# The out projection of a gated layer in seven half-depth products, with stationary weights and moving h

## The chip, the cores and the metric

One core of a Trainium2 chip runs the whole program. The metric is device time in microseconds, lower is better. Times are given as the median of the runs; the profile is of one more execution.

## The reference

Performer attention over 8 batches, 8 heads, 576 positions and head size 64 is followed by a gated feed-forward layer over all 4608 tokens, all in float32:

```python
q_p, k_p = phi(q_s), phi(k_s)              # random features, 128 of them
kv = einsum('bhsm,bhsd->bhmd', k_p, v)
num = einsum('bhsm,bhmd->bhsd', q_p, kv); den = ...
x = num / den                              # laid out as (4608, 512)
xn = x / sqrt(mean(x * x) + 1e-06) * rms_g
g = xn @ w_gate                            # (4608, 512) @ (512, 1536)
val = xn @ w_val
out = (g * sigmoid(g) * val) @ w_out       # (4608, 1536) @ (1536, 512)
```

The weights come as float64-like raw words of 8 bytes and are turned into float32 on the chip. Each float32 operand of a matmul is split into a high part (rounded to the matmul's float32r type) and a low part (the rest), and each product takes three matmuls: high x high, high x low, low x high (`three_pass`).

## The kernel before, in words

Tokens are cut into 12 blocks of 384 (`NBLK`, `TB`), DFF = 1536 into 12 rows of 128 (`NF`), DM = 512 into 4. There are three stages.

Stage A does the attention, normalises x, transposes it (`xT`, and a copy in HBM, `xn_scratch`) and computes the first six rows f of the gated layer (`gated`, `FA` = 6) in ordinary products: weights stationary, 384 tokens moving. Each h row goes to HBM, `h_scratch`. In the same stage `weights(n)` loads all 36 weight tiles of 128 x 512, turns them into float32 on ScalarE and VectorE, and keeps the first 12 split in SBUF. The next 12 pass through `sums`: four sums and differences of their halves are made on VectorE (`sr`), and the seven left-hand factors go to HBM, `lw_scratch`. The last 12, the rows of w_out, are stored as they are to `wo_scratch`.

Stage B computes the other six rows of gate and value (`right`, `left`, `unit`) by the Strassen-Winograd scheme: blocks are taken in pairs (`bp`, six of them), and a 2 x 2 arrangement (two row halves of the product, two halves of the contraction, two blocks) is made with seven products of half the depth in place of eight. `ORDER` lists which left factor meets which right factor. `right` loads four quarters of xn, makes the differences t1 to t4 on VectorE and splits the seven right factors with `halve`: a high part cast by ScalarE, a low part subtracted by VectorE. The results are the R tiles, one pair (high, low) for each of the seven names. `unit` runs the seven products of 6 matmuls each, into three PSUM banks a, b, c; ScalarE copies partial results m1, m5, u2 out of PSUM, VectorE adds them to later ones (`total`). Silu and the product of gate and value follow, and h goes to `h_scratch`.

Stage C is the out projection in ordinary products. `out_weights(f)` loads row f of w_out from HBM and splits it: row 0 into the pool wo0, the others into wo. `out_tile(blk, f)` loads h of one block and row (128 x 384), splits it, and makes 9 matmuls: for each of three groups of 128 tokens, h is stationary and 512 columns of w_out move, three passes, into a PSUM bank that is summed over f. After f = 11 the three banks are copied out (VectorE, ScalarE) and stored as rows of the output.

SBUF is laid out in groups of pools (`GROUPS`). Groups named in `RIGHT` are laid from the top end downwards, the others from the bottom upwards. The very first on the right is "edge", a tile of 8 floats that nobody uses. `change` frees groups and enters new ones in the same place when the items it lists are done: `to_b` and `in_b` lead to stage B. For stage C `to_c` replaces "sources" (xn quarters, raw left factors) by "first" once the last right factors are made, and `in_c` replaces "products" (with the left factors lw of units 1 to 5) by "last" once everything of stage B is done, its last store included. Left factors of unit 0 lie on the right, in lw0, inside the group "operands", as do the R tiles.

The order of all engines' work is made by `Plan` when the program is built: every item has an engine, an assumed duration, items it comes after, a key (smaller first) and buffers that it takes and gives back; a list simulation emits the instructions in the order in which they would begin. Each engine then runs its own instructions strictly in that order, and all loads and stores are issued by SP.

Of the kernel before, what the change touches and what calls it, by code (L numbers as in the profile page):

```python
# [9 lines left out]
F32 = mybir.dt.float32  # L10
F32R = mybir.dt.float32r
AF = mybir.ActivationFunctionType
ALU = mybir.AluOpType
# [16 lines left out]
FA = 6  # L30
# [54 lines left out]
LAND = 2.2  # L85
# [3 lines left out]
class Plan:  # L89
# [95 lines left out]
def performer_glu_kernel(  # L185
# [11 lines left out]
    xn_d: bass.AP,  # L197
    h_d: bass.AP,
    lw_d: bass.AP,
    wo_d: bass.AP,  # L200
):
    nc = tc.nc
    ve = nc.vector
# [53 lines left out]
    def tile_(pool, shape, name, dtype=F32, tag=None):  # L257
        return pools[pool].tile(shape, dtype, tag=tag or pool, name=name)
# [7 lines left out]
    def weights(n, key):  # L266


        if n < 2 * NF:
            src = wgv[n // 2, n % 2]  # L270
        else:
            src = wout[n - 2 * NF]
        t = {}

        def load():
# [56 lines left out]
        if n >= 2 * FA:  # L332

            st["wt", n] = t
            if n >= 2 * NF:

                def store():
                    nc.sync.dma_start(wo_d[n - 2 * NF], t["w"])

                i = st["wo", n - 2 * NF] = add("SP", 0.26 / RATE, store, [i], key, land=LAND)  # L340
                add("NONE", 0, lambda: None, [i], give=[("w", n)])
            else:
                st["w", n] = i
                if n % 4 > 1:
                    sums(n, key)
            return
        f, j = n // 2, n % 2

# [15 lines left out]
    def sums(n, key):  # L364

        un = (n - 2 * FA) // 4 * 2 + n % 2
        t = {}

        def add_up(i):
            def go():  # L370
                if i == 0:
                    t["s"] = tile_("sr", [P, 4, 2 * P], f"sr{un}")
                a, b, s = st["wt", n - 2]["w"], st["wt", n]["w"], t["s"]
                half = slice(0, 2 * P), slice(2 * P, DM)
                x, y, op = (
                    (b[:, half[0]], b[:, half[1]], ALU.add),
                    (s[:, 0], a[:, half[0]], ALU.subtract),
                    (a[:, half[0]], b[:, half[0]], ALU.subtract),
                    (a[:, half[1]], s[:, 1], ALU.subtract),
                )[i]  # L380
                ve.tensor_tensor(out=s[:, i], in0=x, in1=y, op=op)

            return go

        def store(i):
            def go():
                if i == 0:
                    a = st["wt", n - 2]["w"]
                    nc.sync.dma_start(lw_d[un, :, 0:2], a.rearrange("p (i k) -> p i k", i=2))
                elif i == 1:  # L390
                    nc.sync.dma_start(lw_d[un, :, 2], st["wt", n]["w"][:, 2 * P : DM])
                else:
                    nc.sync.dma_start(lw_d[un, :, 3:7], t["s"])

            return go

        after = [st["w", n - 2], st["w", n]]
        ends = [add("SP", size / RATE, store(i), after[i : i + 1], key, land=LAND) for i, size in ((0, 0.26), (1, 0.13))]
        for i in range(4):
            after = [add("DVE", 0.42, add_up(i), after, key, [] if i else [("sr", un)])]  # L400
        ends.append(add("SP", 0.52 / RATE, store(2), after, key, land=LAND))
        st["lw", un] = ends
        add("NONE", 0, lambda: None, ends, give=[("w", n - 2), ("w", n), ("sr", un)])

    def features(tag, c, key):

# [476 lines left out]
    def unit(bp, fp, j, key):  # L883
# [63 lines left out]
        p4 = mm(5, "c", [p3], True)  # L947
        c11 = total("c11", "c", "m1", [p4, m1], [("psB", at, "c"), ("m1", at)])
        p6 = mm(6, "a", [p4, c22], False)
        st["t", bp, un] = t  # L950
        for nm, done in (("c12", c12), ("c22", c22), ("c11", c11), ("c21", p6)):
            src = "a" if nm == "c21" else nm
# [41 lines left out]
    for bp in range(NBLK // 2):  # L994
        for un in range(NU):
            unit(bp, un // 2, un % 2, base + NU * bp + un)

    to_c = change(users("sources"), ["sources"], ["first"])
    in_c = change(list(range(to_c)), ["products"], ["last"])

    def out_weights(f, key):
        t = {}

        def load():
            t["raw"] = tile_("wst", [P, DM], f"oraw{f}")
            nc.sync.dma_start(t["raw"], wo_d[f])

        def hi(part="h"):
            if (f, part) not in lw:
                pool = pools["wo" if f else "wo0"]  # L1010
                lw[f, part] = pool.tile([P, DM], F32R, name=f"o{part}{f}")
            return lw[f, part]

        ready = [in_c if f else to_c]
        i = add("SP", 0.26 / RATE, load, [st["wo", f], to_c], key, [("wst", f)], land=LAND)
        raw = lambda: t["raw"]
        st["o", f] = halve("DVE", hi, lambda: hi("l"), raw, key, [i] + ready, DM, give=[("wst", f)])

    def out_tile(blk, f, key):
        t = {}  # L1020
        at = (blk, f)

        def load():
            t["raw"] = tile_("hin", [P, TB], f"hC{blk}_{f}")
            nc.sync.dma_start(t["raw"], h_d[blk, :, f])

        def hi():
            if "h" not in t:
                t["h"] = tile_("hs", [P, TB], f"hh{blk}_{f}", F32R)
                t["l"] = tile_("hs", [P, TB], f"hl{blk}_{f}", F32R)  # L1030
            return t["h"]

        def product():
            if f == 0:
                st["po"] = [tile_("psB", [P, DM], f"po{blk}_{c}") for c in range(NC)]
            for c in range(NC):
                cs = slice(c * P, (c + 1) * P)
                three_pass(
                    nc,
                    st["po"][c],  # L1040
                    [(t["h"][:, cs], t["l"][:, cs], lw[f, "h"], lw[f, "l"])],
                    start=(f == 0),
                    stop=(f == NF - 1),
                )
            st["po", blk] = st["po"]

        def leave_psum(c):
            def go():
                t["o"] = tile_("o", [P, DM], f"o{blk}_{c}")
                if c % 2 == 0:  # L1050
                    ve.tensor_copy(t["o"], st["po", blk][c])
                else:
                    nc.scalar.copy(t["o"], st["po", blk][c])
                t["o", c] = t["o"]

            return go

        def store(c):
            r0 = blk * TB + c * P
            return lambda: nc.sync.dma_start(out[r0 : r0 + P, :], t["o", c])  # L1060

        i = add("SP", 0.2 / RATE, load, [st["hs", at], to_c], key, [("hin", at)], land=LAND)
        i = halve("DVE", hi, lambda: t["l"], lambda: t["raw"], key, [i], TB, [("hs", at)], [("hin", at)])
        take = [("psB", blk, c) for c in range(NC)] if f == 0 else []
        before = [st["made"]] if "made" in st else []
        i = add("PE", 2.06, product, before + [i, st["o", f]] + ([in_c] if f else []), key, take, [("hs", at)])
        st["made"] = i
        if f == NF - 1:
            for c in range(NC):
                eng, dur = ("ACT", 0.6) if c % 2 else ("DVE", 0.7)  # L1070
                ps, o = ("psB", blk, c), ("o", blk, c)
                n = add(eng, dur, leave_psum(c), [i], key - 1000, [o], [ps])
                add("SP", 0.26 / RATE, store(c), [n], key - 1000, give=[o], land=LAND)

    base = 12000
    for f in range(NF):
        out_weights(f, base + f)
    for blk in range(NBLK):
        for f in range(NF):
            out_tile(blk, f, base + blk * NF + f + 0.5)  # L1080
# [69 lines left out]
```

## Time and profile before

| | us |
|---|---|
| median of 3 runs | 1181.23 (1179.86 to 1181.67) |
| the profiled execution | 1181.44 |
| its span, first to last instruction | 1177.9 |
| busy: TensorE / VectorE / ScalarE / GpSimd | 1161.9 / 674.7 / 580.2 / 131.8 |
| mean granted TensorE clock | 0.998 |
| stage A, to the first product of stage B | 0 to 600.3 |
| stage B, to the first product of stage C | 600.3 to 869.3 |
| stage C, to the end of the span | 869.3 to 1177.9 |

How to read it: the execution's own time is 3.5 us longer than the span of its instructions. A matmul's busy time is its latency, and matmuls overlap, so the pace of TensorE is read from the starts of neighbouring matmuls and not from their durations. A line of the profile can be that of a helper (`three_pass` has L179 to L181, `halve` L789 and L794), and the tile's name tells the use: po is the out projection, pa, pb, pc are the products of stage B, ff those of stage A.

### The profile page before, as it was taken

The page shows a single profiled execution, that of the slowest core. Times are in us where ns is not written, and L with a number is a line of the kernel's source. Part 1 is how long each engine was busy: PE and PEld are TensorE (multiplying, and loading weights), DVE is VectorE, ACT ScalarE, POOL GpSimd, SP SyncE. Part 2 cuts the span into 40 slices and gives each one's busy share as a digit, 9 for nine tenths or more (in the row PEclk, how much of TensorE's full clock was granted, in tenths as well). Part 3 has the DMA queues.
Part 4 walks back from the last instruction along what each step waited for, and adds up shares of the span by engine and source line. Part 5 has one row for each costly group of instructions (what it writes and reads, how often), then busy time and mean ns, then how long its engine had stood idle before and what let it go on. Part 6 is the DMA issues. An engine that isn't in the chain of part 4 may idle for free.

```text
span 1177.9 us, 19998 instructions
## 1 busy us (share of the span) xinstructions
PE 1161.9 (99%) x7433; PEld 1067.4 (91%) x7433; DVE 674.7 (57%) x1390; ACT 580.2 (49%) x1418; POOL 131.8 (11%) x170
## 2 busy tenths in 40 slices
PE   9999999999999999999989999999999999999998
PEld 6898999999999999999989999999988888888886
DVE  4889887998787755547324664664553333333332
ACT  5777777766755655545145454454442222222221
POOL 0133111020201111224144000000000000000000
PEclk9999999999999999999999999999999999999999
DMA  8665585686565633316223331331444444444442
GB/s 285 222 206 176 175 257 178 195 266 212 168 207 170 204 109 100 96 62 222 85 67 106 106 107 63 100 107 54 161 128 135 121 121 147 121 121 121 121 121 86
DMA packets 98032, 171.14 MB, mean 145 GB/s; under 512 B 9360, under 2 KB 65552, under 8 KB 97936
## 3 DMA queue, kind: packets, MB, share of 16 engines
q1 hardware_dynamic: 97712, 169.58, 45.2%
q8 instruction: 58, 0.95, 0.3%
q10 hardware_dynamic: 224, 0.30, 0.1%
q14 instruction: 38, 0.31, 0.1%
HBM read 114.00 MB, written 55.84 MB: 144 GB/s over the span
## 4 chain that ended last, share of the span: by engine, by line
PE 51%; DVE 2%; DMA 0%; issue 0%; ACT 0%; ACTq 0%; DVEq 0%
PE po L180 9%; PE po L179 8%; PE po L181 8%; PE pa L179 4%; PE pa L181 4%; PE pa L180 4%; PE pb L181 2%; PE pb L180 2%; PE pb L179 2%; PE ff L179 1%; PE ff L181 1%; PE ff L180 1%; PE pc L181 1%; PE pc L180 1%; PE pc L179 1%; DMA h_scratch<-h 0%
## 5 line engine op out<-in xcount | busy, mean ns | idle before, releaser
L179 PE MATMUL ff<-xhi,whi 128*128 128x384 f32 x576 | 200.5, 348 | 2.7 <-DVE u L720 2.7
L181 PE MATMUL ff<-xhi,wlo 128*128 128x384 f32 x576 | 193.1, 335 | 0.0
L180 PE MATMUL ff<-xlo,whi 128*128 128x384 f32 x576 | 192.8, 335 | 0.0
L794 DVE TENSOR_TENSOR hl<-hC,hh 128x384 fp32r<-128x384 f32 x144 | 80.2, 557 | 186.4 <-ACT hh L789 186.4
L179 PE MATMUL po<-oh,hh 128*128 128x512 f32 x432 | 170.3, 394 | 1.4 <-ACT oh L789 1.4
L789 ACT CAST hh<-hC 128x384 fp32r<-128x384 f32 x144 | 74.1, 515 | 196.8 <-PE po L180 195.3
L180 PE MATMUL po<-ol,hh 128*128 128x512 f32 x432 | 170.3, 394 | 0.2 <-DVE ol L794 0.2
L181 PE MATMUL po<-oh,hl 128*128 128x512 f32 x432 | 170.1, 394 | 0.0
L179 PEld LDWEIGHTS ff<-xhi,whi 128*128 128x128 f32 x576 | 108.2, 188 | 6.5 <-DVE u L720 3.7
L180 PEld LDWEIGHTS ff<-xlo,whi 128*128 128x128 f32 x576 | 108.4, 188 | 0.0
L181 PEld LDWEIGHTS ff<-xhi,wlo 128*128 128x128 f32 x576 | 108.1, 188 | 0.0
L179 PEld LDWEIGHTS po<-oh,hh 128*128 128x128 f32 x432 | 80.8, 187 | 21.6 <-ACT oh L789 1.8
L180 PEld LDWEIGHTS po<-ol,hh 128*128 128x128 f32 x432 | 80.8, 187 | 20.1 <-DVE ol L794 0.5
L181 PEld LDWEIGHTS po<-oh,hl 128*128 128x128 f32 x432 | 80.8, 187 | 19.8
L463 ACT ACTIVATE qp<-pjq,biq 128x128 f32<-128x128 f32 x288 | 80.7, 386 | 17.4 <-DVE biq L454 14.8
L463 ACT ACTIVATE kp<-pjk,bik 128x128 f32<-128x128 f32 x288 | 79.8, 388 | 18.5 <-DVE bik L454 14.0
L662 POOL TENSOR_TENSOR xlo<-xr,xhi 128x512 fp32r<-128x512 f32 x36 | 47.2, 1312 | 323.5 <-ACT xhi L659 323.5
L716 ACT ACTIVATE t<-ff 128x384 f32<-128x384 f32 x72 | 35.4, 491 | 90.1 <-PE ff L181 90.1
L924 DVE TENSOR_TENSOR c<-pb,u 128x384 f32<-128x384 f32 x36 | 20.0, 556 | 88.4 <-PE pb L181 82.9
L593 PE MATMUL nu<-kv,qpT 128*128 128x65 f32 (+1 forms) x640 | 68.8, 264 | 0.0
L593 PEld LDWEIGHTS nu<-kv,qpT 128*128 128x128 f32 (+1 forms) x640 | 66.2, 181 | 2.4 <-issue 0.6
L720 DVE SCALAR_TENSOR_TENSOR u<-t,ff 128x384 f32<-128x384 f32 x72 | 39.6, 550 | 48.4 <-ACT t L716 48.0
(145 smaller groups left out, 2254.5 us busy)
## 6 DMA issues: line engine op xcount, KB each, us to landing
hC<-h_scratch SPq DMA_DIRECT2D x144, 192.0 KB, 2.4
ink<-in_kx_dram SPq DMA_DIRECT2D x36, 512.0 KB, 4.3
inq<-in_qx_dram SPq DMA_DIRECT2D x36, 512.0 KB, 4.0
h_scratch<-h SPq DMA_DIRECT2D x72, 192.0 KB, 1.9
h_scratch<-c SPq DMA_DIRECT2D x72, 192.0 KB, 1.9
f<-in_wgv_dram SPq DMA_DIRECT2D x24, 512.0 KB, 3.9
xn_scratch<-xr SPq DMA_DIRECT2D x36, 256.0 KB, 2.8
Xb<-xn_scratch SPq DMA_DIRECT2D x24, 384.0 KB, 3.6
```

The source lines that it names most:

```text
L179: nc.tensor.matmul(out, lhsT=ah, rhs=bh, start=first, stop=False, skip_group_check=again)
L180: nc.tensor.matmul(out, lhsT=ah, rhs=bl, start=False, stop=False, skip_group_check=again)
L181: nc.tensor.matmul(out, lhsT=al, rhs=bh, start=False, stop=last, skip_group_check=again)
L463: nc.scalar.activation(st[tag + "p", c][:, h, :], t["pts"][h % 2][:, h // 2, :], AF.Exp, bias=t["bi"][:, h : h + 1], scale=SCALE,)
L593: nc.tensor.matmul(pt[lo:hi, i, :], lhsT=t["qpT"][:, h, lo:hi], rhs=st["kv", b][:, h, :], start=True, stop=True,)
L662: nc.gpsimd.tensor_tensor(out=st["xT", blk][1][:, :, cs], in0=t["xr"], in1=st["xT", blk][0][:, :, cs].bitcast(F32), op=ALU.subtract,)
L716: nc.scalar.activation(t["t"], t[0], AF.Tanh, scale=0.5)
L720: ve.scalar_tensor_tensor(out=t["u"], in0=t["t"], scalar=1.0, in1=t[0], op0=ALU.add, op1=ALU.mult)
L789: h = add("ACT", 0.1 + size / 970, lambda: nc.scalar.copy(hi(), raw()), after, key, take)
L794: e.tensor_tensor(out=lo(), in0=raw(), in1=hi().bitcast(F32), op=ALU.subtract)
L924: ve.tensor_tensor(out=t[name], in0=t[bank], in1=t[y], op=ALU.add)
```

## The change

Stage C is made by the scheme of stage B. The left-hand, stationary factors are combinations of quarters of w_out (rows f and f + 6 are the two halves of the contraction, columns 0 to 255 and 256 to 511 the two row halves of the result). They are made by `sums` in stage A, which now serves both sets of weights, stores three quarters as they are and the four sums together, and for w_out writes them to `wl_scratch`; rows f and f + 6 are loaded one after the other. The right-hand, moving factors are quarters of h of a pair of blocks, [128, 2 rows, 384] at a time (index g, three for each quarter), loaded by `out_right`, with differences t1 to t4 on VectorE, t1, t3 and t4 in place of their sources. Each is split with `halve` into one of the seven R tiles, which are taken in turn. `out_weights(n)` loads the factor of product n (all six f at once) and splits it: product 0 into the tiles of lw0, once unit 0 of the last pair is done, the others into "last". `out_pair` makes, for each product and each g, 6 matmuls of 384 columns for each of two column groups u; ScalarE copies k1, k5, k2 and the last result out of PSUM, VectorE adds the other three. The result is the output transposed, stored as 128 x 384 pieces; the host turns it back. The edge tile grows from 8 to 24 floats.

```diff
-    pools["edge"].tile([P, 8], F32, name="edge")
+    pools["edge"].tile([P, 24], F32, name="edge")
...
-    "first": {"hin": (6, 1), "hs": (3, 2), "wst": (4, 1), "wo0": (1, 1)},
-    "last": {"wo": (1, 1), "o": (3, 1)},
+    "first": {"hb11": (3, 1), "hb12": (3, 1), "hb22": (3, 1), "ht2": (3, 1), "wst": (2, 1)},
+    "last": {
+        "wo": (1, 1), "hb21": (3, 1), "k1": (2, 1), "k5": (2, 1), "k2": (2, 1), "o": (6, 1),
+    },
...
-            src = wout[n - 2 * NF]
+            src = wout[(n - 2 * NF) // 2 + NU * (n % 2)]
...
+            if n < 2 * NF and n % 4 > 1:
+                sums(n - 2, n, (n - 2 * FA) // 4 * 2 + n % 2, key)
+            elif n >= 2 * NF and n % 2:
+                sums(n - 1, n, (n - 2 * NF) // 2, key)
...
         def store(i):
             def go():
+                if i < 3:
+                    a11, a12, _, a22 = parts()
+                    to = wl_d[i, :, un] if out else lw_d[un, :, i]
+                    nc.sync.dma_start(to, (a11, a12, a22)[i])
+                elif out:
+                    nc.sync.dma_start(wl_d[3:7, :, un].rearrange("i p k -> p i k"), t["s"])
...
+    def out_weights(n, key):
+        i = ORDER[n][0]
+        size = 1 if n == 0 else 2
+        def load():
+            t["raw"] = tile_("wst", [P, NU, 2 * P], f"oraw{i}")
+            nc.sync.dma_start(t["raw"], wl_d[i])
...
+            deps = [ld, st["lw0"] if n == 0 else in_c]
+            e = halve("DVE", ..., deps, size * 2 * P)
...
+    def out_right(bp, key):
+        place = {"t1": "b11", "t3": "b12", "t4": "t2"}
...
+        def halves(n, g, after):
+            k = (NBLK // 2 * 7 + 21 * bp + 3 * n + g) % 7
+            slot = "R" + ORDER[k][1]
...
+        for g in gs:
+            halves(0, g, [ld["b11", g]])
+        for g in gs:
+            sub("t1", g, "b12", "b11", [ld["b12", g], e["b11", g]], 2.5)
+            halves(1, g, [d["t1", g]])
+        for g in gs:
+            sub("t2", g, "b22", "t1", [ld["b22", g], d["t1", g]], 4)
+            halves(2, g, [d["t2", g]])
...
+    def out_pair(bp, key):
+        def product(n, u, g, bank, first):
...
+                for k in range(2):
...
+                    pairs.append((wh, wl, r["h"][:, k], r["l"][:, k]))
+                three_pass(
+                    nc, t[bank, u], pairs, start=first, stop=(g == NU // 2 - 1), again=True
+                )
...
+        banks = "ababaca"
+        for n in range(7):
+            for g in range(NU // 2):
+                for u in range(2):
+                    deps = [st["RO", bp, n, g]]
+                    if bp == 0:
+                        deps += [st["o", n, 2 * g], st["o", n, 2 * g + 1]]
...
-    args.append(nc.dram_tensor("out_0_dram", (B * S, DM), F32, kind="ExternalOutput").ap())
+    args.append(nc.dram_tensor("out_0_dram", (DM, B * S), F32, kind="ExternalOutput").ap())
...
-    return r.results[0]["out_0_dram"]
+    return np.ascontiguousarray(r.results[0]["out_0_dram"].T)
```

More of the change, by code (lines that the diff above doesn't have):

```diff
@@ L395, in store @@
             return go
-        after = [st["w", n - 2], st["w", n]]
-        ends = [add("SP", size / RATE, store(i), after[i : i + 1], key, land=LAND) for i, size in ((0, 0.26), (1, 0.13))]
+        after = [st["w", m], st["w", n]]
+        ends = [add("SP", 0.4, store(i), after, key, land=LAND) for i in range(3)]
         for i in range(4):
[L400 to L403, printed above, removed]
+            after = [add("DVE", 0.42, add_up(i), after, key, [] if i else [("sr", m)])]
+        ends.append(add("SP", 0.52 / RATE, store(3), after, key, land=LAND))
+        st["wl" if out else "lw", un] = ends
+        add("NONE", 0, lambda: None, ends, give=[("w", m), ("w", n), ("sr", m)])
     def features(tag, c, key):
@@ L996, in performer_glu_kernel @@
             unit(bp, un // 2, un % 2, base + NU * bp + un)
+    st["lw0"] = st["lw0", NBLK // 2 - 1]
     to_c = change(users("sources"), ["sources"], ["first"])
     in_c = change(list(range(to_c)), ["products"], ["last"])
-    def out_weights(f, key):
+    lo_w = {}
+    def out_weights(n, key):
         t = {}
+        i = ORDER[n][0]
+        size = 1 if n == 0 else 2
         def load():
[L1005 to L1017, printed above, removed]
@@ new lines, in load, with piece @@
+            nc.sync.dma_start(t["raw"], wl_d[i])
+        after = [x for f in range(NU) for x in st["wl", f]] + [to_c]
+        ld = add("SP", 0.79 / RATE, load, after, key, [("wst", n)], land=LAND)
+        ends = []
+        for f0 in range(0, NU, size):
+            def piece(part, f0=f0):
+                if (n, f0, part) not in lo_w:
+                    if n == 0:
+                        w = pools["lw0"].tile(
+                            [P, 1, 2 * P], F32R, tag=f"lw0_{f0}{part}", name=f"o{part}{i}_{f0}"
+                        )
+                    else:
+                        w = pools["wo"].tile([P, 2, 2 * P], F32R, name=f"o{part}{i}_{f0}")
+                    lo_w[n, f0, part] = w
+                return lo_w[n, f0, part]
+            deps = [ld, st["lw0"] if n == 0 else in_c]
+            raw = lambda f0=f0: t["raw"][:, f0 : f0 + size]
+            e = halve(
+                "DVE", lambda p=piece: p("h"), lambda p=piece: p("l"), raw,
+                key + 0.01 * f0, deps, size * 2 * P,
+            )
+            for f in range(f0, f0 + size):
+                st["o", n, f] = e
+            ends.append(e)
@@ new lines, in out_pair, with go, copy @@
+    def out_pair(bp, key):
+        t = {}
+        def product(n, u, g, bank, first):
+            def go():
+                if first:
+                    t[bank, u] = tile_("psB", [P, DM], f"q{bank}_{bp}_{u}")[:, :TB]
+                r = st["ro", bp, n, g]
+                pairs = []
+                for k in range(2):
+                    f = 2 * g + k
+                    f0 = f if n == 0 else 2 * g
+                    wh, wl = (
+                        lo_w[n, f0, p][:, f - f0, u * P : (u + 1) * P] for p in "hl"
+                    )
+                    pairs.append((wh, wl, r["h"][:, k], r["l"][:, k]))
+                three_pass(
+                    nc, t[bank, u], pairs, start=first, stop=(g == NU // 2 - 1), again=True
+                )
+            return go
+        def copy(name, bank, u):
@@ L1063, in out_tile @@
[L1063 to L1073, printed above, removed]
@@ L1075, in performer_glu_kernel, with finish, go @@
-    base = 12000
[L1076 to L1080, printed above, removed]
+                t[name, u] = tile_(name, [P, TB], f"{name}_{bp}_{u}")
+                nc.scalar.copy(t[name, u], t[bank, u])
+            return go
+        def finish(nm, bank, y, u):
+            def go():
+                o = t[nm, u] = tile_("o", [P, TB], f"o{nm}_{bp}_{u}")
+                if y is None:
+                    nc.scalar.copy(o, t[bank, u])
+                else:
+                    ve.tensor_tensor(out=o, in0=t[bank, u], in1=t[y, u], op=ALU.add)
+            return go
```

185 lines of the change are left out of this document (129 added, 56 removed).

## The prediction

> **What bounds the kernel now.** I read the engine table first, then the chain of waits, then busy time by stretches cut where the stages change.
>
> ```profile
> span 1177.9 us, 19998 instructions
> PE 1161.9 (99%) x7433; PEld 1067.4 (91%) x7433; DVE 674.7 (57%) x1390; ACT 580.2 (49%) x1418; POOL 131.8 (11%) x170
> PE 51%; DVE 2%; DMA 0%; issue 0%; ACT 0%; ACTq 0%; DVEq 0%
> ...
> 300.00:420.00 120.00, 120.00 (x945) 116.71 (x945) 94.34 (x219) 71.45 (x186) 20.44 (x27) 1.00 0.57 183
> 600.30:650.00 49.70, 46.01 (x252) 45.26 (x253) 17.26 (x29) 30.27 (x72) 26.50 (x35) 0.97 0.31 104
> 650.00:869.32 219.32, 219.32 (x1261) 218.95 (x1261) 124.39 (x205) 96.98 (x183) 0.00 (x0) 1.00 0.29 96
> 869.32:896.66 27.34, 25.71 (x109) 20.23 (x109) 14.39 (x25) 12.18 (x24) 0.00 (x0) 1.00 0.54 161
> 896.66:1173.45 276.79, 276.79 (x1189) 222.04 (x1187) 85.90 (x152) 72.29 (x142) 0.00 (x0) 1.00 0.41 121
> ```
>
> The stretches list length, then busy time and count of PE, PEld, DVE, ACT, POOL, then clock and DMA. TensorE is never idle for long, the clock is full, and the chain names hardly anything but matmuls. So time is the number of matmuls times the spacing from start to start. The out projection runs from 869.32 to 1173.45: 27.34 + 276.79 = 304.1 us for 1296 matmuls of 512 columns. Stage B, already in seven half-depth products, has 1512 of 384 columns.
>
> ```profile
> 650.01 0.35 PE L179 MATMUL pb<-Rt1h,lw_3h 128*128 128x384 f32 x1
> 650.20 0.34 PE L180 MATMUL pb<-Rt1l,lw_3h 128*128 128x384 f32 x1
> 650.37 0.34 PE L181 MATMUL pb<-Rt1h,lw_3l 128*128 128x384 f32 x1
> 650.55 0.33 PE L179 MATMUL pb<-Rt1h,lw_3h 128*128 128x384 f32 x1
> 650.73 0.33 PE L180 MATMUL pb<-Rt1l,lw_3h 128*128 128x384 f32 x1
> ...
> 672.09 0.34 PE L179 MATMUL pa<-Rb11h,lw_0h 128*128 128x384 f32 x1
> 679.37 0.34 PE L179 MATMUL pa<-Rb11h,lw_0h 128*128 128x384 f32 x1
> ...
> 879.62 0.40 PE L181 MATMUL po<-oh,hl 128*128 128x512 f32 x1
> 896.42 0.40 PE L181 MATMUL po<-oh,hl 128*128 128x512 f32 x1
> ...
> 897.36 0.39 PE L179 MATMUL po<-oh,hh 128*128 128x512 f32 x1
> 898.72 0.39 PE L179 MATMUL po<-oh,hh 128*128 128x512 f32 x1
> ```
>
> These rows of the timeline carry the spacings. 672.09 and 679.37 are the first matmuls of two neighbouring units, 42 matmuls apart: 173.3 ns each. From 879.62 to 896.42 lie 72 steps of the out projection: 233.3 ns. From 897.36 to 898.72 lie six: 226.7 ns. So 128 more columns cost 53.3 ns, and 13.3 ns a matmul do not depend on its width; most out-projection matmuls pay 6.7 ns on top.
>
> Where do the 6.7 ns come from? The six fast steps are those of row f = 0, whose weights (wo0) lie in a right-hand pool; the others' lie in wo, left-hand. In the built kernel left-hand tiles of stages B and C start at multiples of 128 bytes, and right-hand ones 64 bytes off, since 32 bytes of "edge" lie above them. Write each pair as (moving, stationary), modulo 128: out projection f > 0 is (0, 64), f = 0 is (64, 64); stage B is (64, 0) for units 1 to 5 and (64, 64) for unit 0. Only (0, 64) costs the 6.7 ns. A change from (64, 0) to (64, 64) stretches four spacings: 650.01 to 650.73 is 0.72 us where four make 0.693, so 27 ns once.
>
> **The change part by part.** *Matmuls.* Seven products x 6 row tiles x 2 column halves x 3 passes = 252 per pair of blocks, six pairs: 1512, at N = 384. At 173.3 ns that is 262.1 us against 304.1, **-42.0 us**, if nothing waits. Fewer columns (580,608 against 663,552) would make 0.875 of the time; 262.1/304.1 is 0.862, because the 6.7 ns and 2.2 us of waits at the old start (next fence) go too, less the 13.3 ns on 216 more matmuls.
>
> *Alignment.* The edge grows from 32 to 96 bytes, every right-hand tile moves 64, and all pairs of stages B and C become (0, 0). The trace has no such pair. Bounds: the three good readings, and stage A whose two operands both stand 32 off, at 173.3 (rows below), say equal offsets are the cheap case; the one bad reading, +6.7 ns, also is the only one with a moving operand at 0. I take **173.3**, nearest to (64, 64) and (32, 32), and keep ±6.7 ns on 3024 matmuls, ±20.2 us, for the rivals. The 27 ns stretches go: some 20 of them, **-0.5**.
>
> ```profile
> 590.11 0.33 PE L179 MATMUL ff<-xhi,whi 128*128 128x384 f32 x1
> 599.30 0.34 PE L181 MATMUL ff<-xhi,wlo 128*128 128x384 f32 x1
> ...
> 872.96 0.50 PE L179 MATMUL po<-oh,hh 128*128 128x512 f32 x1 [1.40 <-ACT oh L789]
> 873.69 0.50 PE L180 MATMUL po<-ol,hh 128*128 128x512 f32 x1 [0.23 <-DVE ol L794]
> ...
> 870.21 1.91 DMA h_scratch<-c
> 872.29 0.63 ACT oh L789
> 872.94 0.70 DVE ol L794
> ```
>
> (53 steps between the first two: 173.4 ns.) The Trainium skill (TensorE: Matmul & The Clock Gate, Part 2) says the stationary and the moving operand come through two independent read ports, so that loading weights takes nothing from a running matmul; the 6.7 ns, which depend on the pair, do not fit that. The Trainium skill (same page, Back-to-back issue gap) gives N/2.4 + 2.5 ns, 162.5 ns at 384 columns, which no pair here reaches; were the aligned pair to reach it, the sum below would be lower by 10.8 ns x 3024 = 32.7 us, an estimate by that page.
>
> *The start of stage C.* The last rows are the chain there: the last store of stage B lands at 872.1, only then do the pools change, and wo's first tile is cast and split. TensorE lost 2.2 us. Now product 0 has its weights in lw0's tiles (free after unit 0 of the last pair, 869.3 - 5 x 7.28 = 832.9) and h in the R tiles, which come free product by product in the last unit, every 1.04 us from 862.0 + 1.04 = 863.1; its 36 matmuls are 6.2 us of cover, to 875.5. Product 1's first weights can be ready at 872.3 + 0.62 + 0.69 = 873.6. The cover holds; without it, the old 2.2 us.
>
> *Supply of h.* This is the new load.
>
> ```profile
> L849 DVE TENSOR_TENSOR Xt<-Xb,Xt 128x768 f32<-128x768 f32 x12 | 11.9, 989 | 0.2
> L794 DVE TENSOR_TENSOR Rb11l<-Xb,Rb11h 128x768 fp32r<-128x768 f32 x6 | 5.7, 958 | 14.1 <-ACT Rb11h L789 14.1
> L794 DVE TENSOR_TENSOR Rb21l<-Xb,Rb21h 128x768 fp32r<-128x768 f32 x6 | 6.4, 1064 | 0.0
> L789 ACT CAST Rt4h<-Xt 128x768 fp32r<-128x768 f32 x6 | 5.0, 840 | 1.7 <-PE pa L180 1.7
> L924 DVE TENSOR_TENSOR c<-pb,u 128x384 f32<-128x384 f32 x36 | 20.0, 556 | 88.4 <-PE pb L181 82.9 <-ACT lw_3h L789 4.7 <-DMA oraw<-wo_scratch 0.4
> L917 ACT COPY m<-pa 128x384 f32<-128x384 f32 x36 | 17.3, 480 | 52.3 <-PE pa L181 52.2
> L794 DVE TENSOR_TENSOR ol<-oraw,oh 128x512 fp32r<-128x512 f32 x12 | 8.1, 690 | 8.6 <-ACT oh L789 8.6
> L789 ACT CAST oh<-oraw 128x512 fp32r<-128x512 f32 x12 | 7.2, 618 | 10.0 <-DMA h_scratch<-c 6.4 <-DMA oraw<-wo_scratch 3.5
> ```
>
> Per pair VectorE has 21 low halves x 0.96 + 12 differences x 0.99 + 6 totals x 0.56 = 35.4 us; ScalarE 21 casts x 0.84 + 8 copies x 0.48 = 21.5; TensorE 252 x 0.1733 = 43.7. So VectorE fills 81% of each pair, and the seven R slots hold 14.6 us of matmuls ahead. In steady state TensorE sets the pace.
>
> Not in the first pair. Three-quarters of stage C's weights are split then too: 18 x 0.69 = 12.4 us on VectorE, which cannot start before 872. Count VectorE from 864.2 (first R tile free at 863.1, its cast 0.84, some 0.2 for the hand-overs): product 0's low halves 2.9 and stage B's last seven totals 3.9, done at 871.0; product 1, 3 x (0.69 + 0.99 + 0.96) = 7.9, at 878.9; product 2 at 886.8; product 3 (no difference) 4.95, at 891.8; product 4 at 899.7; a pair of totals 1.1; product 5 at 905.7; totals 1.1; product 6 at 914.7, or 915.8 if totals go first. TensorE wants the last third of product n at 869.3 + 6.24n + 4.16: 879.7, 886.0, 892.2, 898.4, 904.7, 910.9. It is late by 0.8 at product 2, 1.3 by product 4 and **4 us** by product 6. Lower end 0.5 (VectorE starts earlier), upper 8 (handshakes with ScalarE 10% longer). In the second pair VectorE's 8 us of slack pays it back.
>
> *PSUM.* Copies and totals of 0.48 and 0.56 have one whole product, 6.24 us, before their bank is written again: nothing.
>
> *Loads and stores.* Weights of one product are 768 KB into two buffers; half as much takes 3.6 us and 512 KB 4.5, so I estimate 6 to 7 us, with two products' time to come: nothing. Bytes per pair: 12 loads of 384 KB and 8 stores of 192 KB, 6.3 MB in 43.7 us, 144 GB/s where the first rows show 217 moved under full TensorE.
>
> ```profile
> wr<-lw_scratch SPq DMA_DIRECT2D x6, 512.0 KB, 4.5
> Xb<-xn_scratch SPq DMA_DIRECT2D x24, 384.0 KB, 3.6
> ...
> 0.00:300.00 300.00, 296.36 (x2461) 270.90 (x2461) 243.69 (x562) 218.21 (x623) 51.05 (x68) 1.00 0.67 217
> ...
> L338 SPq DMA_DIRECT2D wo_scratch<-w x12: 319/320/424, 339.9 to 416.4; - x12
> L838 SPq DMA_DIRECT2D Xb<-xn_scratch x24: 319/320/577, 535.8 to 787.7; - x24
> L381 DVE TENSOR_TENSOR sr<-w x6: 417/422/426, 196.5 to 334.5; 128x256 f32<-128x256 f32 x6
> ```
>
> *Sums of the out weights.* 24 adds x 0.42 = 10.1 us on VectorE; SP issues 24 stores in place of 12 and, for the gate and value weights, 24 in place of 18: 18 x 0.32 = 5.8 us more. All this lies near 340 to 480. From 300 to 420 VectorE has 94.3 of 120 us busy and TensorE all of it, and stage B's first loads, which wait until these tiles are given up, go out at 535.8. Hidden; without cover 10 us. I add **+0.5** for a reshuffled order, ends -1 and +5.
>
> *The end.* A ScalarE copy of 0.48 and 192 KB replace a VectorE copy of 0.69 (L1051, 128x512) and 256 KB: **-0.3**.
>
> Sum: 1181.4 (the profiled execution, 0.2 above the median 1181.23) - 42.0 - 0.5 + 4.0 + 0.5 - 0.3 = **1143 us**; with its ends 1137 to 1152.
>
> **The rivals.** (a) *Aligned pairs are cheaper than any seen*: if the step from (0, 64) to (64, 64) happens once more, 6.7 ns x 3024: 1123. For it: 13.3 ns remain unexplained in every spacing. Against: three different pairs share exactly this value, like a floor. By the Trainium skill's gap, cited above, it would be 1110, an estimate.
>
> (b) *The moving operand at 0 is what costs*: +6.7 ns x 3024, stage B slows too: 1163. For it: the only slow pair has it. Against: an effect of one operand would hardly let the weights' offset leave its mark in the 27 ns stretches.
>
> (c) *VectorE becomes the bound in every pair.* It needs 8.3 us more than 35.4; with all low halves at 1.06, as Rb21l's mean, it is 37.5, still short. At 48 us per pair: 1143 + 6 x 4.3 = 1169.
>
> (d) *Slower than before: each low half waits out its cast.* If VectorE cannot start a half until its own cast is done and the cast does not run ahead, a pair takes 21 x (0.84 + 0.96) + 11.9 + 3.3 = 53.0 us: 318 against 304.1, with weights split in series (24 pieces, near 28 us) in the first pair 1195 to 1223. It decides from 304.1/6 = 50.7 us a pair. Against: before Rb21l VectorE stood idle 0.0 us, so casts run ahead; with seven slots they can again.
>
> **How the numbers follow.** Forecast 67%, (a) 14%, (b) 8%, (c) 7%, (d) 4%. The range 1119 to 1158 holds the forecast, most of (a) and the mild end of (c); (b), (d) and the far ends of (a) and (c) stay out, some 20%. The forecast's own range is 1137 to 1152. A measurement here tells 0.2%, 2.4 us; all but (d) are faster: 0.96, 0.01, 0.03.
>
> **What would show it.** Right: 1512 matmuls of 384 columns in stage C spaced 173.3 ns; stage B as before without stretched spacings; idle time before matmuls only in the first pair of C, released by VectorE's low halves or weights, about 4 us; no wait for a copy or total; stage B starting near 600. Wrong: a spacing of 166.7 or 180.0 in B and C alike (a, b); idle time before matmuls in every pair (c, d); stage B starting several us later.

## The result, and the profile after

| | before | after |
|---|---|---|
| median of 4 runs each, us | 1180.74 (1179.86 to 1181.67) | 1144.08 (1143.85 to 1145.20) |
| ratio | | 0.9691, interval 0.9675 to 0.9708 |
| profiled execution, us | 1181.44 | 1143.85 |
| its span, us | 1177.92 | 1142.07 |

The forecast was 1143.0 with a range of 1119 to 1158. (The kernel before has one run more here than in its own table.) The page of the changed kernel, its engine table and chain by engine:

```profile
span 1142.1 us, 20442 instructions
PE 1124.3 (98%) x7649; PEld 1088.7 (95%) x7649; DVE 793.0 (69%) x1492; ACT 628.5 (55%) x1448; POOL 130.5 (11%) x170
PE 48%; DVE 2%; DMA 1%; ACT 0%; issue 0%; ACTq 0%; DVEq 0%
```

TensorE lost 38 us of busy time, VectorE gained 118, and the chain is still one of matmuls. The same stretches as before, cut at the new borders (columns as in the prediction), and the two stretches of matmuls in which the granted clock was halved:

```profile
600.03:650.00 49.97, 45.98 (x245) 45.21 (x246) 16.25 (x28) 29.50 (x71) 26.36 (x35) 0.93 0.30 100
650.00:866.62 216.62, 216.62 (x1250) 216.59 (x1250) 124.14 (x205) 99.22 (x189) 0.00 (x0) 1.00 0.33 110
866.62:915.00 48.38, 44.43 (x242) 43.22 (x242) 43.70 (x62) 28.40 (x46) 0.00 (x0) 0.96 0.68 220
915.00:1138.50 223.50, 223.50 (x1291) 223.34 (x1289) 166.62 (x197) 103.25 (x144) 0.00 (x0) 1.00 0.42 122
...
605.40:612.23 6.83, 6.07 (x19) 6.07 (x20) 0.56 (x1) 5.72 (x15) 6.57 (x11) 0.50 0.20 56
881.90:885.31 3.41, 3.41 (x12) 3.41 (x12) 3.41 (x6) 1.37 (x3) 0.00 (x0) 0.50 0.51 141
```

TensorE is idle at two places only: early in stage B, as before, and in the first pair of stage C (866.62 to 915.00). From 915 to the end there is no pause. Its spacing, from the timeline:

```profile
672.02 0.33 PE L181 MATMUL pa<-Rt4h,lw_2h 128*128 128x384 f32 x1
679.30 0.34 PE L181 MATMUL pa<-Rt4h,lw_2h 128*128 128x384 f32 x1
...
1000.00 0.33 PE L183 MATMUL qc<-hRb21h,ol 128*128 128x384 f32 x1
1012.48 0.33 PE L183 MATMUL qa<-hRb11h,ol 128*128 128x384 f32 x1
...
875.98 0.33 PE L181 MATMUL qb<-hRt1h,oh 128*128 128x384 f32 x1
...
1138.32 0.34 PE L183 MATMUL qa<-hRt4h,ol 128*128 128x384 f32 x1
```

In stage B 42 steps take 7.28 us, in stage C 72 take 12.48: 173.3 ns in both. What TensorE waited for between 600 and 915 (the waits view: total, times, longest; a sixth row of 0.2 us is left out):

```profile
PE pa L181 <- ACT m L922: 3.8, 1, 3.8
PE qa L182 <- DVE hRt4l L799: 1.9, 1, 1.9
PE qb L182 <- DVE hRt1l L799: 1.3, 1, 1.3
PE pa L181 <- issue: 0.7, 1, 0.7
PE qb L181 <- ACT hRt1h L794: 0.6, 1, 0.6
```

Measured from start to start of matmuls, over a step of 173.3 ns, the first is 3.95 us (before: 3.57), and those of stage C are 0.74 and 1.57 (product 1), 0.29 (product 4) and 2.10 (product 6): 4.7 us.

The spans differ by 35.85 us, which divides at matmul starts like this. Stage B begins 0.30 earlier. Stage B with product 0, 1548 matmuls to 875.98, takes 7.6 us over 173.3 ns each; before, the 1512 of stage B took 6.9 over: +0.7. Products 1 to 6 of all pairs, 1476 matmuls to the step after 1138.32, take 262.5 us, 6.7 over 255.8; so stage C costs 262.1 + 6.7 = 268.8 against 304.1: -35.3. From the last matmul's step to the end of the span it is 3.58 instead of 4.50: -0.9. Outside the span the profiled execution of before had 3.52 us and that of after 1.78: -1.7 more, 37.6 in all.

### The profile page after: what moved, and what is told of

Its sections match the earlier page's. It is cut to its first block, busy times and chain, and to the rows that moved or that the text cites. A ratio compares the mean times of both kernels' runs of the same rounds, so it can differ in the third digit from the quotient of the medians.

```text
span 1142.1 us, 20442 instructions
## 1 busy us (share of the span) xinstructions
PE 1124.3 (98%) x7649; PEld 1088.7 (95%) x7649; DVE 793.0 (69%) x1492; ACT 628.5 (55%) x1448; POOL 130.5 (11%) x170
## 4 chain that ended last, share of the span: by engine, by line
PE 48%; DVE 2%; DMA 1%; ACT 0%; issue 0%; ACTq 0%; DVEq 0%
PE pa L181 4%; PE pa L182 4%; PE pa L183 4%; PE qa L182 4%; PE qa L183 4%; PE qa L181 4%; PE qb L182 2%; PE pb L182 2%; PE pb L183 2%; PE pb L181 2%; PE qb L183 2%; PE qb L181 2%; PE ff L181 1%; PE ff L182 1%; PE qc L182 1%; PE ff L183 1%
## 5 line engine op out<-in xcount | busy, mean ns | idle before, releaser
L721 ACT ACTIVATE t<-ff 128x384 f32<-128x384 f32 x72 | 35.3, 491 | 91.8 <-PE ff L183 91.8
L731 DVE SCALAR_TENSOR_TENSOR h<-u,ff 128x384 f32<-128x384 f32 x72 | 39.8, 553 | 42.9 <-PE ff L183 40.4
L549 PE MATMUL kvp<-v,kp 128*128 128x65 f32 x512 | 58.8, 275 | 0.0
L549 PEld LDWEIGHTS kvp<-v,kp 128*128 128x128 f32 x512 | 58.4, 192 | 0.4
L451 DVE TENSOR_REDUCE mxk<-pjk 128x4 f32<-128x512 f32 x72 | 46.8, 685 | 9.7 <-PE pjk L439 9.6
L451 DVE TENSOR_REDUCE mxq<-pjq 128x4 f32<-128x512 f32 x72 | 46.9, 684 | 7.7 <-PE pjq L439 7.5
L590 ACT COPY qpT<-qt 128x512 f32<-128x512 f32 x72 | 39.4, 587 | 20.5 <-PE qt L587 19.8
L967 ACT ACTIVATE c<-c 128x384 f32<-128x384 f32 x54 | 28.4, 526 | 39.4 <-DVE c L929 39.3
L922 ACT COPY m<-pa 128x384 f32<-128x384 f32 x36 | 17.3, 481 | 55.2 <-PE pa L183 55.2
```

Source lines behind the costliest of these rows:

```text
L451: ve.tensor_reduce(out=by_half[:, i, :], in_=t["pts"][i], axis=AX.X, op=ALU.max)
L549: nc.tensor.matmul(t["pt"][:, i, :], lhsT=st["kp", c][:, h, :], rhs=st["v", c][:, h, :], start=(n == 0), stop=(n == 3),)
L590: nc.scalar.copy(t["qpT"][:, 4 * half : 4 * half + 4, :], t["pt", half])
L721: nc.scalar.activation(t["t"], t[0], AF.Tanh, scale=0.5)
L731: ve.scalar_tensor_tensor(out=t["h"], in0=t["u"], scalar=0.5, in1=t[1], op0=ALU.mult, op1=ALU.mult)
```

## The experiments

Two questions stood. First, is it the pair of offsets (moving at 0, stationary at 64, modulo 128) that costs 6.7 ns a matmul (theory A), or the moving operand's offset alone, or the pool the weights lie in? And does the enlarged edge, which is part of the change, bring anything? Second, what makes the 4.7 us of waits at the start of stage C: VectorE, which has more to make for the first pair than time (theory V), or the heads of ScalarE's and VectorE's queues (the instruction that each has to run next), which stand behind stage B's last store ahead of the weights' casts (theory Q)?

**1. The kernel before, with the larger edge alone.**

```diff
-    pools["edge"].tile([P, 8], F32, name="edge")
+    pools["edge"].tile([P, 24], F32, name="edge")
```

> The kernel before with the edge tile at 24 floats in place of 8 and nothing else: every pair of matmul operands of stages B and C now stands at (moving 0, stationary 0) modulo 128 bytes. Theory A, the offset of the stationary operand against an aligned moving one costs the 6.7 ns: the out projection falls from 233.3 to 226.7 ns a matmul, 1188 x 6.7 = 7.9 us, and stage B loses its stretches (0.5 us): 1172.4 us, ratio 0.993. Theory B, the 6.7 ns come from where the weights lie (left end of SBUF) or from a moving operand at 0: 233.3 stays, 0 to -0.5 us.

Measured: 1171.53 us (1170.98 to 1173.93), ratio 0.9925, interval 0.9909 to 0.9942. Two out-projection matmuls 72 steps apart, f > 0:

```profile
939.96 0.39 PE L180 MATMUL po<-ol,hh 128*128 128x512 f32 x1
956.28 0.39 PE L180 MATMUL po<-ol,hh 128*128 128x512 f32 x1
```

16.32 us, 226.7 ns a step in place of 233.3. The weights, which move here, stayed in their pool at 0; h, stationary, came from 64 to 0, and the 6.7 ns went from all 1188 matmuls that had them (7.9 us of the 8.3 gained). So neither the weights' pool nor a moving operand at 0 is what costs.

**2. The changed kernel with the old edge** (24 back to 8, so that the pairs are moving 64, stationary 0, and 64 for both in unit 0 and product 0).

> The changed kernel with the edge back at 8 floats: pairs (64, 0) for units 1 to 5 and products 1 to 6, (64, 64) for unit 0 and product 0. Theory A: all spacings stay 173.3 ns, only the four stretched spacings at each change of pair return: about +0.5 us, 1144.6, so the alignment is worth nearly nothing to this change. Rival, aligned pairs carry part of the gain: 180.0 ns in the products with unequal offsets, up to +17 us.

Measured: 1144.22 us (1141.87 to 1146.68), ratio 0.9695, interval 0.9673 to 0.9718. The mean spacing from 960 to 1125 us is 173.45 ns, and 173.33 in the changed kernel. The stretches at changes of the offsets are all the difference: 0.1 us in stage C from the second pair on, and 0.4 us in stage B from 615 us on (0.60 over 173.3 ns a step, against 0.17 in the changed kernel). The alignment is worth 8 us to the old layout and nothing that can be measured to the new one, since exchanging the operands had already left the slow pair.

**3. The changed kernel with its left-hand pools shifted by 64 bytes.** This makes the slow pair with the new operands (a tile of 16 floats ahead of the left factors of units 1 to 5 and of products 1 to 6).

```diff
     "products": {
+        "padB": (1, 1),
...
     "last": {
+        "padC": (1, 1),
```

> The changed kernel with an unused tile of 64 bytes ahead of the left-hand pools of stages B and C: the stationary operands of units 1 to 5 and products 1 to 6 stand at 64, the moving ones at 0; unit 0 and product 0 stay (0, 0) as a control in the same run. Theory A, the pair (0, 64) costs 6.7 ns at any width: 180.0 ns on 1260 + 1296 matmuls, +17.0 us, 1161. Rival, it costs only 512 columns: 173.3 everywhere, +0.

Measured: 1148.61 us (1146.92 to 1151.79), ratio 0.9736, interval 0.9718 to 0.9753. **3b. The same with 32 bytes** (8 floats), in a single execution.

> As the one before with 32 bytes: pairs (0, 32). If the cost is by the distance to the next multiple of 128: more or less than 6.7 ns by the distance (3.3 or 10 ns, +8 to +25 us); if by any unequal offset: 180.0 ns, +17 us; if it needs an offset of 64: 173.3, +0.

Measured: 1140.37 us. Rows 42 steps apart in stage B and 72 apart in stage C for 64 bytes, then 42 apart for 32:

```profile
668.58 0.34 PE L185 MATMUL pc<-Rb21h,lw_1l 128*128 128x384 f32 x1
676.00 0.34 PE L185 MATMUL pc<-Rb21h,lw_1l 128*128 128x384 f32 x1
987.10 0.34 PE L183 MATMUL qb<-hRb22h,oh 128*128 128x384 f32 x1
999.82 0.34 PE L183 MATMUL qc<-hRb21h,oh 128*128 128x384 f32 x1
```

```profile
667.59 0.34 PE L185 MATMUL pc<-Rb21h,lw_1l 128*128 128x384 f32 x1
674.87 0.34 PE L185 MATMUL pc<-Rb21h,lw_1l 128*128 128x384 f32 x1
```

With 64 bytes 176.7 ns in both stages, with 32 bytes 173.3; product 0 of the run with 64 bytes, which kept (0, 0), stays at 173.4. So the pair (0, 64) costs here too, though 3.3 ns and not 6.7; why it costs half as much with 384 columns as with 512 stays open. Both profiled executions have the same waits in stage B (1.7 us), and differ by 8.6 us: stage B begins 0.5 us later with 64 bytes and takes 3.1 longer, the first pair of stage C takes 1.5 longer with a second stretch of half clock, and the other five pairs 3.5, where 1080 shifted matmuls x 3.3 ns make 3.6.

**4. The low parts of the out weights (products 1 to 6) on GpSimd.**

```diff
-                "DVE", lambda p=piece: p("h"), lambda p=piece: p("l"), raw,
+                "POOL" if n else "DVE", lambda p=piece: p("h"), lambda p=piece: p("l"), raw,
```

> The changed kernel with the low parts of the out weights of products 1 to 6 made by GpSimd, idle in stage C, in place of VectorE: 18 x 0.69 = 12.4 us leave VectorE's queue in the first pair. Theory V, VectorE's supply makes the waits at 878 to 881, 901 and 912 to 914 us (5 us of waiting, and 1.4 us of half clock after the first): they go, but product 1's first weights come 0.6 us later (GpSimd 1.3 in place of 0.69): 5 to 6 us less, 1138 to 1139. Theory Q, ScalarE's casts of h stand behind the casts of weights that wait for stage B's last store: the wait at 878 to 881 stays, only the later ones go: 2.5 us less, 1141.5.

Measured: 1144.68 us (1143.88 to 1145.57), ratio 0.9699, interval 0.9684 to 0.9713: nothing gained. VectorE's timeline, GpSimd's group from 866 to 916 us, and TensorE's waits:

```profile
870.76 0.95 DVE L1066 TENSOR_TENSOR ht<-hb,hb 128x768 f32<-128x768 f32 x1
871.63 2.05 DVE L1066 TENSOR_TENSOR hb<-hb,hb 128x768 f32<-128x768 f32 x1
```

```profile
L799 POOL TENSOR_TENSOR ol<-oraw,oh 128x512 fp32r<-128x512 f32 x18 | 34.2, 1930 | 244.8 <-DMA hb<-h_scratch 238.1 <-ACT oh L794 6.7
```

```profile
PE qb L182 <- DVE hRb22l L799: 3.0, 1, 3.0
PE qb L182 <- DVE hRt1l L799: 2.5, 1, 2.5
```

GpSimd begins at 871.50, and from then on the same subtraction takes VectorE 2.05 us instead of 0.95. The Trainium skill (SBUF — State Buffer, Who interferes with whom) says that a VectorE instruction with two SBUF inputs contends with a GpSimd instruction that reads SBUF; these rows agree, with a factor of 2.2 on VectorE. So 12 us were taken off VectorE's list and it still became later: the run doesn't decide between V and Q.

**5. The weights later in the order**: those of product 1 behind the second h tile of product 1, those of product n behind the last h tile of product n - 1. This takes the weights' casts out of the queue heads (the h tiles are also listed before the weights).

```diff
             deps = [ld, st["lw0"] if n == 0 else in_c]
+            if n:
+                deps.append(st["RO", 0, max(1, n - 1), 1 if n == 1 else 2])
```

> The changed kernel with the weights of product 1 ordered after the second h tile of product 1, and those of product n after the last h tile of product n - 1: ScalarE and VectorE are not held by the weights' wait for stage B's last store. Theory Q: VectorE's 1.8 us and ScalarE's 6.5 us of waiting at 868 to 875 are filled, the wait at 878 to 881 goes: 3 to 4 us less. Theory V: the same work in another order; the weights come later in place of h, the first wait moves to the start of product 1 and the sum changes by less than 1.5 us.

Measured: 1139.63 us (1138.55 to 1144.27), ratio 0.9663, interval 0.9640 to 0.9686. The waits of the profiled execution, which was the slowest of the four, from 866 to 920 us:

```profile
PE qb L181 <- ACT oh L794: 2.5, 1, 2.5
PE qa L182 <- DVE hRt4l L799: 0.7, 1, 0.7
```

The wait at product 6 falls from 1.9 to 0.7, but the first one now is for the weights themselves, at the start of product 1: from start to start 2.7 and 0.9, 3.6 us in all against 4.7. That is what V expected of the waits, and from the first matmul of stage C to that of the second pair it takes 53.5 us as in the changed kernel's profile, with 6.83 us of half clock in place of 3.41. The median, 4.5 us lower, is nearer to Q, but run 8 gives the changed kernel itself 1140.02, so the times decide nothing.

**6. The start of stage B**: the left factors of units 1 to 5, whose casts wait for stage A's last store at the head of ScalarE's queue, behind the first two copies of unit 0.

```diff
-    for un in range(NU):
+    left(0, base)
+    unit(0, 0, 0, base)
+    in_b = st["m5", 0, 0]
+    for un in range(1, NU):
         left(un, base + un)
```

> The changed kernel with the left factors of units 1 to 5 ordered after the first two copies out of PSUM of stage B (m1, m5 of unit 0). In both kernels ScalarE casts four tiles of unit 1 ahead of m1 after the wait for stage A's last store, and TensorE waits 3.6 to 3.9 us and then has half its clock for 3.4 or 6.8 us. Theory: the copy starts 1.2 us earlier, the gap falls to 2.7 us, the clock stays full: 1.2 + 2.4 to 2.9 = 3.6 to 4.1 us less, 1140. Rival, the gap is still long enough for the clock: 1.2 us less and half clock for 3.4 us.

Measured: 1138.98 us (1137.67 to 1140.24), ratio 0.9648, interval 0.9632 to 0.9664. ScalarE:

```profile
602.76 0.48 ACT L922 COPY m<-pa 128x384 f32<-128x384 f32 x1 [3.70 <-PE pa L183]
605.29 0.41 ACT L794 CAST lw_0h<-wr 128x256 fp32r<-128x256 f32 x1 [1.15 <-DMA h_scratch<-h]
```

The copies no longer stand behind the casts, the 3.8 us wait is 0.9, and no half clock follows it. The median is 5.1 us under that of the result and 1.0 under that of run 8, where the changed kernel had the short wait without this edit: what the edit takes away is the dependence on the store, which is a late one here (see 8). Stage C keeps 4.5 us of waits.

**7. Numbers 4, 5 and 6 together:**

> The three edits together (GpSimd for the low parts of the out weights, h first, left factors after the first copies). If each works on waits of its own: 1144.1 - 5.5 - 4 = 1134 to 1136; if the order of h and weights is worth nothing beside GpSimd's help, 1135 to 1137; if GpSimd's slower halves make product 1 wait, 1138 or more.

Measured: 1143.21 us (1142.44 to 1143.63), ratio 0.9685, interval 0.9671 to 0.9700. The third case came: GpSimd's slow low parts make product 1 wait (the row below, 6.1 us). The half clock had set in before, behind a wait of 2.6 us for product 1's first weights, and lasted 10.24 us.

```profile
PE qb L183 <- POOL ol L799: 6.1, 1, 6.1
```

**8. The changed kernel again**, as a control on one chip with the two that follow.

> The changed kernel, unchanged, beside the two below on the same chip. Both theories: 1144 us again, between 1141 and 1147 by the wait at the start of stage B and the half clock behind it (3.6 to 3.9 us of wait with 3.41 or 6.83 us of half clock, against 1.7 us with none); waits of the first product pair of stage C sum to about 5 us.

Measured: 1140.02 us (1139.20 to 1143.61), ratio 0.9663, interval 0.9631 to 0.9696, below the expectation. Issue of stage A's last store and the first cast that waits for it, in the first profile of this kernel and in this one:

```profile
599.96 0.32 SPq L736 DMA_DIRECT2D h_scratch<-h  x1
604.41 0.40 ACT L794 CAST lw_0h<-wr 128x256 fp32r<-128x256 f32 x1 [6.63 <-DMA h_scratch<-h]
```

```profile
600.28 0.32 SPq L736 DMA_DIRECT2D h_scratch<-h  x1
602.48 0.40 ACT L794 CAST lw_0h<-wr 128x256 fp32r<-128x256 f32 x1 [4.37 <-DMA h_scratch<-h]
```

The same store lets the cast start 4.45 us after its issue, or 2.20. The wait at the start of stage B is 3.95 or 1.69 accordingly; with the half clock behind it stage B is 4.8 us shorter in this execution, which began it 0.3 us later and lost 0.7 more in the first pair of stage C (its waits sum to 5.0 us). That is the 3.8 us between the two profiled executions.

The trace shows what goes with the delay. In the DMA view of the 5 us after the issue, the first profile has one packet of the queue that loads instructions (q8); this run has none, and its store lands sooner:

```profile
q8 instruction: 1, 0.02, 2.2%
h_scratch<-h SPq DMA_DIRECT2D x1, 192.0 KB, 4.1
```

```profile
h_scratch<-h SPq DMA_DIRECT2D x1, 192.0 KB, 1.9
```

So it is in all 13 profiled executions of these kernels: in the eight where such a packet (16 KB, 1.1 to 1.8 us) runs beside the store, 8 of the store's 128 packets start only once it has ended; in the five where none does, no packet of the store is late. Eight of 128 is the share of one of the 16 DMA engines, so these packets probably stood behind the instructions on one engine, but the trace names no engine. Why the load of instructions falls there in some executions is open.

**9. No low part of the weights of products 1 to 6.** Their high tile is used in its place, so the matmuls are the same in number and size, and VectorE is rid of 18 x 0.69 = 12.4 us.

```diff
-            e = halve("DVE", ...)
+            if n == 0:
+                e = halve("DVE", ...)
+            else:
+                e = add("ACT", ..., lambda p=piece, r=raw: nc.scalar.copy(p("h"), r()), deps, ...)
...
-                        lo_w[n, f0, p][:, f - f0, u * P : (u + 1) * P] for p in "hl"
+                        lo_w[n, f0, "h" if n else p][:, f - f0, u * P : (u + 1) * P] for p in "hl"
```

> Leaves out: the low part of the out weights of products 1 to 6; the high tile stands in its place, so the matmuls keep their number and size, and VectorE loses about 6 x 2.07 = 12.4 us of work in the first pair of stage C. Theory V (VectorE has too much to make in the first pair): the waits at 901 us (0.29) and 912 us (2.10) go, and what is left of stage C's waits is under 1.5 us of the 4.7 to 5.2 of the changed kernel; time 1140 to 1141. Theory Q (the wait behind stage B's last store, which ACT's and VectorE's queues meet ahead of the weights' casts, sets all): the 2.3 us at 878 to 881 stay, only the 2.4 us later go; time 1142. If neither: the waits stay at 5 us and 1144.

Measured: 1134.44 us (1132.79 to 1137.67), ratio 0.9613, interval 0.9573 to 0.9652. All the waits of TensorE from 600 to 915, and the head of ScalarE's queue:

```profile
PE pa L181 <- ACT m L922: 3.0, 1, 3.0
PE pa L181 <- issue: 0.7, 1, 0.7
PE pa L181 <- DVE c L929: 0.2, 1, 0.2
```

```profile
871.76 2.19 ACT L1049 CAST oh<-oraw 128x512 fp32r<-128x512 f32 x4 [6.18 <-DMA h_scratch<-c]
```

No wait of stage C is left in this view. (Both theories' times were too high, since they started from 1144 us for the changed kernel, which has 1140.02 beside this run.) ScalarE still stood 6.18 us at its queue's head behind the same store, and that cost TensorE nothing. So ScalarE's queue head makes no wait of its own. VectorE's went too in this run, since VectorE no longer needs the weights; the next one keeps it.

**10. Number 6, and VectorE's work of the first pair begun earlier.** The first difference t1 is written to a tile of its own instead of over b11, so t1 and t3 of the first pair no longer wait for b11's split.

```diff
-        place = {"t1": "b11", "t3": "b12", "t4": "t2"}
+        place = {"t2": "t1", "t3": "b12", "t4": "t2"}
...
-            sub("t1", g, "b12", "b11", [ld["b12", g], e["b11", g]], 2.5)
+            sub("t1", g, "b12", "b11", [ld["b12", g], ld["b11", g]], 2.5)
...
-            sub("t2", g, "b22", "t1", [ld["b22", g], d["t1", g]], 4)
+            sub("t2", g, "b22", "t1", [ld["b22", g], e["t1", g]], 4)
```

> On top of the stage-B order with the left factors of units 1 to 5 behind the m copies of unit 0: the first difference of the h tiles is written to a tile of its own instead of over the loaded one, so that those of the first pair can be made from about 840 us on, in VectorE's idle time: 5.7 us of VectorE's work lie ahead of stage C. Theory V: counted by rows VectorE has product 1 ready at 876.0, 2 at 883.8, 4 at 894.8, 6 at 908.7, each ahead of TensorE (879.7, 886.0, 898.4, 910.9); the waits of 4.5 us fall to under 1, time 1135 (1139 - 4). Theory Q: the wait for the weights at the start of product 1 stays, 1 to 2.7 us, time 1137. If the moved differences delay the left factors of stage B's last unit instead, waits show up ahead of 866 us and it is 1139 or more.

Measured: 1133.23 us (1131.01 to 1133.56), ratio 0.9596, interval 0.9566 to 0.9626. The waits of TensorE from 600 to 915, the stretch that holds most of the first pair (it runs from 860.2 to 907.2 here), and the queue heads:

```profile
PE pa L181 <- issue: 0.7, 1, 0.7
```

```profile
866.62:915.00 48.38, 48.38 (x279) 48.11 (x278) 45.09 (x61) 31.70 (x52) 0.00 (x0) 1.00 0.69 226
```

```profile
868.61 1.14 ACT L794 CAST oh<-oraw 128x512 fp32r<-128x512 f32 x2 [4.43 <-DMA h_scratch<-c]
869.26 1.29 DVE L799 TENSOR_TENSOR ol<-oraw,oh 128x512 fp32r<-128x512 f32 x2 [1.19 <-ACT oh L794]
```

(The 0.7 us put down to issue stands in the view of the changed kernel too.) The weights are all split, both queues still meet the store, and TensorE has no pause and no half clock: with VectorE's work begun earlier, the queue heads cost nothing. V holds; Q alone makes no wait. It is the best version measured: the same work as the changed kernel, with every run below every one of the control's on the same chip (1139.20 to 1143.61). Between the two profiled executions stage B, which number 6 changes, takes 1.8 us less, and from the first matmul of stage C to that of the second pair it takes 47.1 us in place of 54.2 (53.4 in run 6): the earlier differences are worth 6.4 to 7.1 us.

## Why the prediction was right, point by point

**Matmuls: right.** 1512 at 173.3 ns; the forecast -42.0 is what stage C shows from 915 on. Rivals (a) and (b) fall with the spacing: neither 166.7 nor 180.0. The reading that only the pair (0, 64) costs was shown by 1 and 3, and its size at 384 columns, which the prediction took as 6.7, is 3.3; the prices of (a) and (b) were twice too large. The two rules of the Trainium skill cited in the prediction (TensorE: Matmul & The Clock Gate): independent read ports leave a cost of the pair unexplained, 6.7 ns at 512 columns in run 1; the gap of 162.5 ns, which the page gives for an isolated matmul, appears in no run, the lowest is 173.3.

**VectorE in steady state: right.** From 915 to 1138.5 it is busy 166.6 of 223.5 us, 75% (33.2 us, 76%, in a pair from the middle; 81% counted), and TensorE has no pause; (c) and (d) fall. In the seven-slot order casts do run ahead.

**Stretched spacings, -0.5: hidden.** They went, but stage B lost 0.7 us net, since its early wait was 0.4 longer in this execution and the half clock behind it 6.83 us instead of 3.41. Run 8 shows that this wait changes from execution to execution.

**Supply in the first pair, +4.0: the mis-sized step, 6.7.** That the first pair alone would wait, and for VectorE's low halves (hRt1l, hRt4l), was right. That product 1 would be ready in time was not: 2.3 of the 4.7 us of waits stand there. The count failed where it let VectorE start at 864.2 and run without a pause. Its rows:

```profile
865.00 0.96 DVE L799 TENSOR_TENSOR hRb11l<-hb,hRb11h 128x768 fp32r<-128x768 f32 x1 [2.82 <-ACT hRb11h L794]
...
875.12 1.90 DVE L799 TENSOR_TENSOR ol<-oraw,oh 128x512 fp32r<-128x512 f32 x3 [1.80 <-ACT oh L794]
876.93 0.95 DVE L1066 TENSOR_TENSOR hb<-hb,hb 128x768 f32<-128x768 f32 x1
...
881.28 0.95 DVE L799 TENSOR_TENSOR hRt1l<-hb,hRt1h 128x768 fp32r<-128x768 f32 x1
...
916.36 0.95 DVE L799 TENSOR_TENSOR hRt4l<-ht,hRt4h 128x768 fp32r<-128x768 f32 x1
```

It starts 0.8 late and stands 1.80 ahead of the first weights, with differences that need no weights queued behind them; later it stands another 2.8 for a cast of ScalarE and for results of TensorE. Against that, its prices were too high: from 876.93 to 881.28 lie five low halves and differences, 0.87 us each from start to start where the count took 0.96 and 0.99, 3.4 us in all up to product 6. The two errors partly cancel. So product 1 is ready at 882.2 (counted 878.9) and product 6 at 917.3 (914.7), the others 2.3 to 3.0 late. One part of Q is true: the queue head makes VectorE's list 1.8 us later. The prediction had named the store's landing (872.1 before) but used it only as the earliest start of the weights. Now it is later:

```profile
868.05 4.33 SPq L980 DMA_DIRECT2D h_scratch<-c  x4
...
874.47 1.66 ACT L794 CAST oh<-oraw 128x512 fp32r<-128x512 f32 x3 [6.53 <-DMA h_scratch<-c]
```

Of the 6.7 us, 4.7 are waits; the rest lies mainly in the 3.41 us of half clock behind them (12 matmuls 0.32 us apart in place of 0.173, 1.6 us together), which had no term at all.

**The start of stage C: right, with less to spare.** Product 0 covers until 875.98; the first weights of product 1 are cast at 875.1 rather than 873.6.

**Sums, +0.5; the end, -0.3.** Stage B began 0.30 earlier, so the new adds and stores are hidden. The last copy is 0.48 instead of 0.69 us, and the tail 0.9 shorter: 0.2 in the copy, the rest after it, where the smaller store lies.

**What the sum did not have.** 1.7 us lie outside the span, not in the kernel: other executions of the kernel before, in the runs beside these experiments, have 1.8 to 3.2 us there, so 3.52 was high. That and the shorter tail offset the stall: the sum missed by 0.8 us of the profiled execution with single terms off by up to 2.7. That it came so close is partly luck, and run 8 has the same kernel 4.1 us lower, with a shorter wait at the start of stage B. Two slips of the prediction's arithmetic change nothing: the weights that it calls three-quarters are 18 pieces of 21, whose 12.4 us it adds rightly, and the ends of the forecast's own range add up to 1138, not 1137, and 1152.

## What to carry to other kernels

When a scheme moves work from TensorE to an engine with room on average, count that engine's list at the border between stages from its true first free moment, with every wait that stands at its queue's head, and by the time from start to start of its instructions; work that can be made ready before the border (here by not writing a result over its source) was worth 6.4 to 7.1 us here, and moving work to a third engine nothing. Judge an alignment by the pair of operands as they meet after the change: exchanging them had already left the slow pair, and the larger edge brought nothing on top.

## What the runs showed of the hardware

- Operands in float32r with moving at 0 and stationary at 64 modulo 128 bytes cost 6.7 ns a matmul at 512 columns (the kernel before, against run 1) and 3.3 at 384 (run 3); with offsets (0, 0), (64, 0) and (0, 32) a matmul takes the same 173.3 ns at 384.
- Subtractions on GpSimd beside those of VectorE slowed VectorE from 0.95 to 2.05 us; the mean of GpSimd was 1.93 us (run 4).
- The granted clock is halved in stretches of 3.41 us and its multiples (3.41, 6.83, 10.24), after pauses as short as 1.9 us (the wait at product 6 in run 8, while the same wait brought none in the first profile of that kernel); the 3.0 us of run 9 brought none. The Trainium skill (TensorE: Matmul & The Clock Gate, Part 1: The HAM clock gate) tells of a free-running window of 3413 ns and of the lower clock after at least one idle window. The lengths agree; that a pause shorter than a window sufficed does not, and the measurement decides.
- A store of 192 KB, issued alone at the end of stage A, released its waiter after 2.20 us in one execution and after 4.45 in another of the same kernel, where a 16 KB packet of the instruction queue ran beside it.
